# Attention and a SoLU block on one core: w_out handled by halves of its columns, four output tiles in halves, states in four loads, a new order

## The chip, the cores and the metric

The kernel runs on one core of a Trainium2 chip. The core has TensorE for matrix products (PE, with weight loads as PEld), VectorE (DVE), ScalarE (ACT), GpSimd (POOL) and SyncE (SP), which here issues all DMA transfers. Products land in PSUM; everything else lives in SBUF. The metric is the time of one execution on the device in microseconds. The profile is of one execution; a run's time is a little longer than the span from its first to its last instruction.

## What is computed

```python
# attention: x [8, 8, 512, 64], state [8, 8, 32, 64]
scores = scale * np.matmul(x, state.transpose(0, 1, 3, 2))
a = softmax(scores)
xread = np.matmul(a, state)
scores2 = scale * np.matmul(state, x.transpose(0, 1, 3, 2))
a2 = softmax(scores2)
sread = np.matmul(a2, x)
x = concatenate([xread, sread], axis=2)  # as 4352 rows of 512
# SoLU block: w_in [512, 1024], w_out [1024, 512], g_ln [1024]
h = x @ w_in
solu = h * softmax(h)
ln = (solu - mu) / np.sqrt(var + 1e-06) * g_ln
out = ln @ w_out
```

Both softmaxes run over the last axis; `mu` and `var` are those of a row of `solu`. All is float32.

## The kernel before, in words

The 4352 rows are 34 tiles of 128: four for each of eight batches, and tiles 32 and 33 for the state reads. Since `xread` is a product with the states, the kernel multiplies the states into w_in first (`state_w_in`, steps `V`: batch and half of the columns) and then takes h of a tile as softmax weights times that (`h_steps`, `H`). Products that need precision are made of three: each operand is split into a high part in a short float format and a low part (`swh` and `swl`, `ath` and `atl`, `uh` and `ul`, `wohi` and `wolo`), and high x high, high x low and low x high are summed. Batch 0 uses plain float32 operands in h.

A weight arrives as raw 64-bit words (`load_w`, `l`), 16 blocks: `l0` to `l7` are w_in, `l8` to `l15` w_out. ScalarE takes the rounding part (`low_words`, `cl`), VectorE shifts and masks in two operations, and a third operation adds the rounding (`to_f32`, `c`). w_in is used as it is for the states and, turned by small DMAs (`turn_w_in`, `wp`) and split (`split_w_in`, `wi`), for the last two tiles. w_out is split by `split_w_out` (`wo`): high part times g on ScalarE, low part times g on VectorE.

For a batch: load x (`LT`, `Ln`), scores (`S`), softmax over tokens (`E`), over states (`A`, for batch 0 in two parts `Ah`), reads (`R`). The products of w_in and the states of six batches are stored to DRAM (`Y`), loaded again when due (`Z`) and split (`P`). For a tile: h (`H`), the softmax and normalisation (`chain`, `C`: maximum, exponential, product, scaling, square), a transpose of blocks on VectorE, a store to DRAM and a rearranging load (`bounce`, `D`: tiles `ub`, `ut`, `back`), the split (`t_steps`, `T`), and the output product with eviction and store (`o_steps`, `O`): 24 products of 128x512, 48 of 128x256 for tile 33, whose two halves are made apart.

Nothing plans at run time. ORDER is a written list of steps; `issue` takes one piece of the named step per entry. OPT says which engine does the n-th piece of a kind (`a` ScalarE, `d` VectorE, `p` GpSimd). PLACES says which SBUF slot or PSUM bank the n-th tile of a kind gets; a tile that gets a slot waits for the last reader of the tile before it. Each engine then runs its own instructions in that order. SP is one queue too: a transfer that waits there holds up all behind it. `K` is one small product that only keeps TensorE busy.

Of the kernel before, what the change touches and what calls it, by code (L numbers as in the profile page):

```python
# [8 lines left out]
F32 = mybir.dt.float32  # L9
# [19 lines left out]
OPT = dict(ph=2, k4=45, direct=[0, 1], hn=[0], vh=[0, 1], ah=[0], add='dpdpdpdpppppppdp', whi='aadd', wlo='dppp',  # L29
           ev='daaaaaaaadaaadaaaaaaaaaaaaaaaaaa', swh='aaaaaaaaadaaaaaa', swl='pppppppppppdddpd', sub='dppddppd',  # L30
           subh='dpdddpdddpdddpdd', mulh='dddddpdddpdddpdd', mul='ppppdpdd', ath='aaaaaddd', alo='dpppppdp',
           up='aaaaaaaaddaaadaaaaaaaaddaadadadadd',
           uh='aaaaaaaadaaaddaaaaaaaaaaadaadaaadaaadaddaaaadaaddaaddadddadaaadadaaa',
           ul='ppddppppdpdppppppddppdppppddpppdpdpppdppppppppdppppdpppdddddppdddddd',
           oe='aaaaaaaaaaaaaadadaaaadadaaaaadaada', hs='aaaaaaaa', jit=[], ed=[0, 1], ec='aaaaaaaaaaaaaaaa')
# [36 lines left out]
C26 D26 O23*5 O24 R6*2 C27 C26 H28 D26 X D26 T27 C28 X C28*2 O25*3 H31 O25 O27 H31*2 O25*2 H31*2 O23 C28 D28*2 O25*4
O27*2 H31 D28 C25*2 T26 O25*2 T27 O25*2 T26*2 C31*2 H29*3 O27*3 wi2*2 O26 T26 H29*3 C31 O26*6 C31 D31*2 O27*2 O26 C26
O27*4 T28*4 C27 O28*3 O27*2 C28 O28*2 C29 O26*2 C29 O26*2 C29*2 D31 D29 C28 O28*2 T31*2 O28*3 T31*2 H30*4 O26 D29 O26
O28*2 H30*2 H33*3 C30 O31 O28 D29 C30*2 C31 C30*2 D30 O31*3 H33 wi1 H33*8 C33*3 H32 C31 H32*3 O31*3 C33 H32*3 D30*2
T30*3 D33 O31*4 O28 T29 O31*2 H32*4 D33*2 T29*2 H32 O31 C32*2 O30*2 O29*2 C32 T33 O29*3 O30 O29*3 C32 D32*3 O30*4
T33*2 O30*3 T30 O30*2 O29 C30 O30 C33 T29 O30 T33 O33*5 T32 O33*3 O29*3 T32 O33*3 T32 O33 C33 O33*9 O32*6 C29*2 O32*4
T32 O32*2 O33 O29*2 C32*2 O32*2 O33*6
# [25 lines left out]
def attention_then_solu_ffn(ctx, tc, xT, xn, stB, w_in, w_out, g, out):  # L104
# [11 lines left out]
    SLOTS = dict(s2=2, m1=1, z1=1, r=1, sc=2, rr=3)  # L116
# [52 lines left out]
    def load_st(k):  # L169

        st[k] = sbuf("s2", [P, 2 * NP * 2, 2, NS], F32, f"st{k}")
        nc.sync.dma_start(st[k].rearrange("p (k c s) h n -> p k c s (h n)", k=2, c=NP), stB[:, k:k + 2])
        yield

    def state_of(b, head):

        c, h = divmod(head, 2)
        return st[b // 4 * 2][h * D:(h + 1) * D, (b // 2 % 2) * 2 * NP + 2 * c + ((b % 2) ^ (c % 2)), h, :]
# [22 lines left out]
    def load_w(n):  # L201


        raw[n] = block([HALF, 2], U32, f"raw{n}")
        if n < 2 * NP:
            c, half = divmod(n, 2)
            src = w_in[c * P:(c + 1) * P, half * HALF:(half + 1) * HALF]
            nc.sync.dma_start(raw[n], src.bitcast(U32).rearrange("p (f k) -> p f k", k=2))
        else:
            src = w_out.bitcast(U32).rearrange("(p c f) h -> c f p h", p=4, f=NS)[n - 2 * NP]  # L210
            nc.sync.dma_start(raw[n].rearrange("p h k -> p (h k)"), src)
        yield
# [439 lines left out]
```

## Time and profile before

| | us |
|---|---|
| median of 3 runs | 352.25 (350.67 to 353.64) |
| the profiled execution's own time | 350.98 |
| its span | 349.2 |
| granted TensorE clock, mean | 0.995 |

The page gives busy times of each engine and the span in 40 slices; a digit is a tenth of a slice:

```profile
PE   5999999999999999999999999999999999999995
DVE  3889999997888778998779897888787896555720
ACT  3579999889658567578565676555863463544250
POOL 0063594378756764678579463444455518412220
PEclk9899999999999999999999999999999999999999
```

A busy TensorE is not one that does useful work all the time, since the small products of `K` and products that wait inside a group count as busy. So the useful products have to be counted. In an answer that lists instructions in order of time, a row has start, length, engine, line and operation, and in brackets the idle time before it with what ended it. The groups give busy time and the mean of one in ns.

### The profile page before, as it was taken

The numbers are of one execution on the slowest core, as the hardware profiler recorded it, in microseconds if no ns is written. First come the engines' busy times: TensorE is split into PE (matmuls) and PEld (weight loads), VectorE is DVE, ScalarE is ACT, GpSimd is POOL, SyncE is SP. The second block draws the span as 40 slices with busy tenths as digits, with TensorE's granted clock in tenths as the row PEclk, the third lists the DMA queues.
The fourth block names the chain that finished last, engine by engine and source line by source line (L and its number), as shares of the span: only waits on it lengthen the run. The fifth ranks groups of instructions, "written<-read, shape, count | busy, mean of one in ns | idle before, by whom it ended". The sixth has DMA issues, their size and how long they took to land.

```text
span 349.2 us, 6119 instructions
## 1 busy us (share of the span) xinstructions
PE 339.0 (97%) x2220; PEld 255.5 (73%) x2220; DVE 274.9 (79%) x386; ACT 220.6 (63%) x356; POOL 182.7 (52%) x241
## 2 busy tenths in 40 slices
PE   5999999999999999999999999999999999999995
PEld 4343335888788867888878778887888888888894
DVE  3889999997888778998779897888787896555720
ACT  3579999889658567578565676555863463544250
POOL 0063594378756764678579463444455518412220
PEclk9899999999999999999999999999999999999999
DMA  7996998899998899999997976897897345344432
GB/s 240 416 402 268 342 322 269 307 294 343 294 363 272 339 363 332 312 329 310 340 327 263 323 247 215 288 306 288 270 297 255 113 150 212 115 167 172 150 107 75
DMA packets 47854, 94.25 MB, mean 270 GB/s; under 512 B 4432, under 2 KB 26192, under 8 KB 47824
## 3 DMA queue, kind: packets, MB, share of 16 engines
q1 hardware_dynamic: 47824, 93.87, 77.8%
q8 instruction: 17, 0.28, 0.3%
q14 instruction: 13, 0.11, 0.1%
HBM read 54.53 MB, written 37.22 MB: 263 GB/s over the span
## 4 chain that ended last, share of the span: by engine, by line
PE 43%; DVE 20%; DMA 15%; ACT 11%; issue 4%; POOL 4%; SPq 1%; DVEq 0%; ACTq 0%; POOLq 0%
PE o L545 28%; PE h L477 13%; DMA back<-ut 7%; DMA out_dram<-osb 3%; DVE u L490 2%; DMA raw<-w_in_dram 2%; DVE sm L484 2%; ACT u L495 2%; DVE wf L234 2%; DVE ub L514 2%; ACT e L487 2%; ACT uh L142 2%; DMA ut<-ub 2%; POOL ul L147 1%; DVE aT L408 1%
## 5 line engine op out<-in xcount | busy, mean ns | idle before, releaser
L147 POOL TENSOR_TENSOR ul<-back,uh 128x512 fp32r<-128x512 f32 x43 | 58.8, 1373 | 66.4 <-ACT uh L142 40.1
L545 PE MATMUL o<-wohi,uh 128*128 128x512 f32 (+1 forms) x280 | 74.8, 385 | 0.6 <-ACT uh L142 0.4
L545 PE MATMUL o<-wolo,uh 128*128 128x512 f32 (+1 forms) x280 | 75.3, 383 | 0.0
L545 PE MATMUL o<-wohi,ul 128*128 128x512 f32 (+1 forms) x280 | 73.6, 383 | 0.0
L545 PEld LDWEIGHTS o<-wohi,uh 128*128 128x128 f32 x280 | 51.5, 188 | 12.1 <-ACT uh L142 1.3
L545 PEld LDWEIGHTS o<-wolo,uh 128*128 128x128 f32 x280 | 51.8, 188 | 10.4
L545 PEld LDWEIGHTS o<-wohi,ul 128*128 128x128 f32 x280 | 51.7, 188 | 10.3
L490 DVE SCALAR_TENSOR_TENSOR u<-h,e 128x1024 f32<-128x1024 f32 x34 | 41.4, 1217 | 22.1 <-ACT e L487 21.2
L487 ACT ACTIVATE e<-h,sm 128x1024 f32<-128x1024 f32 x34 | 37.9, 1113 | 29.0 <-DVE sm L484 28.7
L514 DVE STREAM_TRANSPOSE ub<-u 128x1024 f32<-128x1024 f32 x34 | 42.1, 1237 | 8.3 <-ACT u L495 7.9
L484 DVE TENSOR_REDUCE sm<-h 128x1 f32<-128x1024 f32 x34 | 41.0, 1207 | 8.5 <-PE h L477 4.6
L502 ACT ACTIVATE e<-u 128x1024 f32<-128x1024 f32 x34 | 35.9, 1056 | 9.5 <-DVE u L497 9.2
L142 ACT ACTIVATE uh<-back 128x512 fp32r<-128x512 f32 x48 | 29.0, 623 | 17.2 <-DMA back<-ut 17.2
L495 ACT ACTIVATE u<-u,sm 128x1024 f32<-128x1024 f32 x24 | 27.6, 1149 | 16.4 <-DVE u L490 16.3
L552 ACT ACTIVATE osb<-o,sm 128x512 f32<-128x512 f32 (+1 forms) x29 | 19.2, 663 | 25.4 <-PE o L545 12.1
L477 PE MATMUL h<-swh,ath 128*128 128x512 f32 x112 | 35.1, 395 | 0.0
L477 PE MATMUL h<-swl,ath 128*128 128x512 f32 x112 | 34.5, 389 | 0.0
L477 PE MATMUL h<-swh,atl 128*128 128x512 f32 x112 | 34.5, 389 | 0.0
L237 POOL TENSOR_TENSOR wf<-wf,r 128x512 uint32<-128x512 uint32 x11 | 14.0, 1290 | 27.7 <-DVE wf L234 23.9
L147 POOL TENSOR_TENSOR swl<-swf,swh 128x1024 fp32r<-128x1024 f32 x10 | 24.3, 2432 | 8.0 <-ACT swh L142 5.2
L477 PEld LDWEIGHTS h<-swh,ath 128*128 128x128 f32 x112 | 20.6, 188 | 5.3 <-ACT e L487 0.8
L477 PEld LDWEIGHTS h<-swl,ath 128*128 128x128 f32 x112 | 21.0, 188 | 4.5
(86 smaller groups left out, 496.8 us busy)
## 6 DMA issues: line engine op xcount, KB each, us to landing
ut<-ub SPq DMA_DIRECT2D x34, 512.0 KB, 3.1
back<-ut SPq DMA_DIRECT2D x34, 512.0 KB, 4.9
out_dram<-osb SPq DMA_DIRECT2D x33, 256.0 KB, 4.7
xT<-xT_dram SPq DMA_DIRECT2D x16, 512.0 KB, 8.0
xn<-xn_dram SPq DMA_DIRECT2D x16, 512.0 KB, 7.7
kept<-vt SPq DMA_DIRECT2D x12, 512.0 KB, 6.3
swf<-kept SPq DMA_DIRECT2D x12, 512.0 KB, 6.3
raw<-w_in_dram SPq DMA_DIRECT2D x8, 512.0 KB, 8.4
```

Source lines behind the costliest of these rows:

```text
L142: nc.scalar.activation(out, src, AF.Copy)
L147: engine(k).tensor_tensor(out=out, in0=a, in1=hi.bitcast(F32), op=ALU.subtract)
L237: engine(of("add", n)).tensor_tensor(out=w, in0=w, in1=rounding[n], op=ALU.add)
L477: nc.tensor.matmul(ph[t][:, cols], left[l][:, p, tok], weights[:, cols], start=(p, l, r) == (0, 0, 0), stop=(p, l, r) == (parts - 1, *kind ...
L484: nc.vector.tensor_reduce(nm, ph[t], AX.X, ALU.max, negate=True)
L487: nc.scalar.activation(e, ph[t], AF.Exp, bias=nm, accum_out=z)
L490: nc.vector.scalar_tensor_tensor(out=u, in0=ph[t], scalar=-1.0, in1=e, op0=ALU.mult, op1=ALU.mult, accum_out=su)
L495: nc.scalar.activation(u, u, AF.Identity, bias=su, scale=-float(DF))
L502: nc.scalar.activation(e, u, AF.Square, scale=float(DF) ** -0.5, accum_out=ss)
L514: nc.vector.transpose(ub, us[t][0])
L545: nc.tensor.matmul(po, ut[t][l][:, f, :], w[NP + f // 2][:, f % 2, cols], start=(hf, l, w is wohi, q) == (0, 0, True, 0), stop=(hf, l, q) ...
L552: nc.scalar.activation(o[:, cols], po, AF.Copy, scale=us[t][1])
```

## The change

Five things:

- The states are loaded in four transfers (256 KB each, one for two batches) in place of two of 512 KB.
- Each of the eight raw blocks of w_out holds half of the columns of two row chunks, in place of all columns of one; it takes two transfers of 256 KB. `l8` to `l11` are the first 256 columns, `l12` to `l15` the others.
- w_out's split is another: first a product with g in place (`wg`: five on VectorE, three on GpSimd), then the high part as a plain copy on ScalarE (`woh`), then the low part as a difference (`wol`: five on VectorE, three on GpSimd). Before, the products with g were part of the other two operations.
- Tiles 0 to 3 make their output in two halves of 256 columns, as tile 33 did. Each half has its own SBUF tile.
- ORDER, PLACES and the engine strings in OPT are new throughout. Counted over the kernel: VectorE adds in `to_f32` 5 to 9, GpSimd's 11 to 7; `uh` on ScalarE 48 to 32, VectorE 20 to 16, GpSimd 0 to 20; all evictions of the state products on ScalarE; `K` 34 to 33.

```diff
-    SLOTS = dict(s2=2, m1=1, z1=1, r=1, sc=2, rr=3)
+    SLOTS = dict(s4=4, m1=1, z1=1, r=1, sc=2, rr=3)
...
-        st[k] = sbuf("s2", [P, 2 * NP * 2, 2, NS], F32, f"st{k}")
-        nc.sync.dma_start(st[k].rearrange("p (k c s) h n -> p k c s (h n)", k=2, c=NP), stB[:, k:k + 2])
+        st[k] = sbuf("s4", [P, NP * 2, 2, NS], F32, f"st{k}")
+        nc.sync.dma_start(st[k].rearrange("p (c s) h n -> p c s (h n)", c=NP), stB[:, k])
...
-            src = w_out.bitcast(U32).rearrange("(p c f) h -> c f p h", p=4, f=NS)[n - 2 * NP]
-            nc.sync.dma_start(raw[n].rearrange("p h k -> p (h k)"), src)
+            half, i = divmod(n - 2 * NP, NP)
+            src = w_out.bitcast(U32).rearrange("(p c f) h -> c f p h", p=4, f=NS)
+            for c in range(2):
+                nc.sync.dma_start(raw[n].rearrange("p (c h) k -> p c (h k)", c=2)[:, c],
+                                  src[2 * i + c, :, :, half * DM:(half + 1) * DM])
...
-        w, by, hi, lo = wf[n][:, q], gT[:, f:f + 1], wohi[n][:, q], wolo[n][:, q]
-        if of("hs", f) == "a":
-            nc.scalar.activation(hi, w, AF.Copy, scale=by)
-        else:
-            nc.vector.tensor_scalar_mul(hi, w, by)
-        yield
-        nc.vector.scalar_tensor_tensor(out=lo, in0=w, scalar=by, in1=hi.bitcast(F32), op0=ALU.mult, op1=ALU.subtract)
+        w = wf[NP + m // 2][:, m % 2].rearrange("p (c h) -> p c h", c=2)
+        engine(of("wg", m)).tensor_tensor(out=w, in0=w, in1=gT[:, 2 * i:2 * i + 2, None].broadcast_to(w.shape), op=ALU.mult)
+        yield
+        hi, lo = (x[NP + i][:, :, half * DM // 2:(half + 1) * DM // 2] for x in (wohi, wolo))
+        copy(of("woh", m), hi, w)
+        yield
+        minus(of("wol", m), lo, w, hi)
...
-        width = DM // 2 if t == NTILES - 1 else DM
+        width = DM // 2 if t in OPT["oh"] else DM
...
-            if at == 0:
-                o = sbuf("o", [P, DM], F32, f"osb{t}")
+            o = sbuf("o", [P, width], F32, f"osb{t}_{at}")
```

Three places of the new order. In the rows a name has its tile or batch number and then a running number (`o1_0_737` is the output of tile 1 from column 0); the engine's rows stand in its order.

TensorE, where the first output product stands. Before, it comes behind h of tiles 4 and 5 (and the reads of batch 0 and the scores of batch 2, further up):

```order
L477 MATMUL h5_706<-swh1_1_439,ath1_660 128x512 x2
L477 MATMUL h5_706<-swl1_1_528,ath1_660 128x512 x2
L477 MATMUL h5_706<-swh1_1_439,atl1_688 128x512 x2
L545 MATMUL o1_0_737<-wohi4_680,uh1_730 128x512 x2
L545 MATMUL o1_0_737<-wohi5_683,uh1_730 128x512 x2
L545 MATMUL o1_0_737<-wolo4_681,uh1_730 128x512 x2
```

Now it comes behind the products of states of batch 7, and with h of tiles 4 and 5 still to do:

```order
L189 MATMUL swps7_1_1_600<-wf3_116,st3_467 32x512 x2
L572 MATMUL warm_92<-ident_74 128x128
L549 MATMUL o1_0_646<-wohi4_384,uh1_609 128x256 x2
L549 MATMUL o1_0_646<-wohi5_545,uh1_609 128x256 x2
L549 MATMUL o1_0_646<-wolo4_385,uh1_609 128x256 x2
L189 MATMUL swps6_0_1_655<-wf0_97,st3_467 32x512 x2
```

The first halves of tiles 1 and 0 moved ahead of h of tiles 4 and 5; their second halves follow it, and then tile 3.

VectorE up to and behind `ub` of tile 2, the last transpose of batch 0. Before, all of w_out's low parts lie ahead of it:

```order
L490 SCALAR_TENSOR_TENSOR u2_678,sm2_649<-h2_603,e2_676 128x1024
L271 SCALAR_TENSOR_TENSOR wolo5_684<-wf5_335,gT_81,wohi5_683 128x512
L234 SCALAR_TENSOR_TENSOR wf7_431<-raw14_366,wf7_431 128x512
L271 SCALAR_TENSOR_TENSOR wolo4_681<-wf4_397,gT_81,wohi4_680 128x512 x2
L271 SCALAR_TENSOR_TENSOR wolo5_684<-wf5_335,gT_81,wohi5_683 128x512
L237 ISA wf7_431<-wf7_431,r14_524 128x1024
L147 TENSOR_TENSOR ul1_732<-back1_658,uh1_730 128x512
L271 SCALAR_TENSOR_TENSOR wolo6_546<-wf6_269,gT_81,wohi6_545 128x512 x2
L271 SCALAR_TENSOR_TENSOR wolo7_743<-wf7_431,gT_81,wohi7_742 128x512
L147 TENSOR_TENSOR ul1_732<-back1_658,uh1_730 128x512
L271 SCALAR_TENSOR_TENSOR wolo7_743<-wf7_431,gT_81,wohi7_742 128x512
L514 STREAM_TRANSPOSE ub2_775<-u2_678 128x1024
```

Now the second halves of w_out are converted ahead of it, and their low parts come behind:

```order
L236 TENSOR_SCALAR wf7_246<-raw15_330 128x512
L239 SCALAR_TENSOR_TENSOR wf6_340<-raw13_441,wf6_340 128x512
L239 SCALAR_TENSOR_TENSOR wf7_246<-raw15_330,wf7_246 128x512
L242 ISA wf6_340<-wf6_340,r13_774 128x1024
L518 STREAM_TRANSPOSE ub2_784<-u2_731 128x1024
L440 TENSOR_TENSOR sr0_821<-srps0_788,sc0_178 128x128
L149 TENSOR_TENSOR wolo4_385<-wf6_340,wohi4_384 128x2x256
L149 TENSOR_TENSOR wolo5_546<-wf6_340,wohi5_545 128x2x256
L242 ISA wf7_246<-wf7_246,r15_724 128x1024
L270 TENSOR_TENSOR wf7_246<-wf7_246,gT_81 128x512
L149 TENSOR_TENSOR wolo6_462<-wf7_246,wohi6_461 128x2x256
```

The low parts of the first halves moved up, between the chains of tiles 1 and 0; those of the second halves moved behind the last `ub` of batch 0.

SP, where tiles 3 and 2 go through DRAM. Before, the load of tile 3 is ahead of the store of tile 2:

```order
L331 DMA ut3_715<-ub3_673 128x1024
L313 DMA swf2_0_727<-kept2_0_434 128x1024
L308 DMA kept5_0_755<-vt5_0_241 128x1024
L336 DMA back3_763<-ut3_715 128x4x256
L248 DMA wp2_781<-wf2_151 32x1024
L331 DMA ut2_797<-ub2_775 128x1024
```

Now it is behind it, and half an output stands there too:

```order
L335 DMA ut3_735<-ub3_733 128x1024
L312 DMA kept7_1_751<-vt7_1_584 128x1024
L561 DMA out_dram<-osb0_0_753 128x256
L335 DMA ut2_786<-ub2_784 128x1024
L340 DMA back3_836<-ut3_735 128x4x256
```

The load `back` of tile 3 moved behind a store that waits for the transpose of tile 2.

More of the change, by code (lines that the diff above doesn't have):

```diff
@@ L27 @@
 NTILES = B * NT + B * NS // P
[L29 to L35, printed above, removed]
@@ L78 @@
-T32 O32*2 O33 O29*2 C32*2 O32*2 O33*6
+OPT = dict(ph=2, k4=45, direct=[0, 1], hn=[0], vh=[0, 1], ah=[0], add='dddddpdpppdppdpd', whi='apdd', wlo='dpdd',
+           ev='aaaaaaaaaaaaaaaaaaaaaaaaaaaaaaaa', swh='aaaaaadaapapaada', swl='ppdppddppppdddpp', sub='dpddpdpp',
+           subh='dpdddpdddpdddpdd', mulh='dpdddpdddpdddpdd', mul='pdpppdpd', ath='aaaaapaa', alo='ddpppppp',
+           up='aaaaaaaadapdaaaaaadaadadaapdadaddd',
+           uh='aaaaaadapapppdaapaaaapaapaadpadpapddaappaapaaadppddapaddapddppadddap',
+           ul='dppdppdppdppdpddpdppppddpppdpdpppppdpppppppdpppdppdpppddddpdpdppdpdp',
+           oe='aaaaaaaaaadaaaaaaaaaaaaaaaaaddddaa', jit=[], ed=[0, 1], ec='aaaaaaaaaaaaaaaa', oh=[0, 1, 2, 3, 33],
+           wg='ddpddppd', woh='aaaaaaaa', wol='dppddddp')
@@ L177, in state_of @@
         c, h = divmod(head, 2)
[L178 removed]
+        return st[b // 2][h * D:(h + 1) * D, 2 * c + ((b % 2) ^ (c % 2)), h, :]
     def all_heads(b, banks, moving, js=range(NJ)):
@@ L257, in split_w_in, with split_w_out @@
         yield
-    def split_w_out(f):
-        n, q = NP + f // 2, f % 2
-        if q == 0:
-            wohi[n] = block([2, DM], F32R, f"wohi{n}")
-            wolo[n] = block([2, DM], F32R, f"wolo{n}")
-        w, by, hi, lo = wf[n][:, q], gT[:, f:f + 1], wohi[n][:, q], wolo[n][:, q]
-        if of("hs", f) == "a":
-            nc.scalar.activation(hi, w, AF.Copy, scale=by)
-        else:
-            nc.vector.tensor_scalar_mul(hi, w, by)
+    def split_w_out(m):
+        half, i = divmod(m, NP)
+        if half == 0:
+            wohi[NP + i] = block([2, DM], F32R, f"wohi{NP + i}")
+            wolo[NP + i] = block([2, DM], F32R, f"wolo{NP + i}")
+        w = wf[NP + m // 2][:, m % 2].rearrange("p (c h) -> p c h", c=2)
+        engine(of("wg", m)).tensor_tensor(out=w, in0=w, in1=gT[:, 2 * i:2 * i + 2, None].broadcast_to(w.shape), op=ALU.mult)
         yield
-        nc.vector.scalar_tensor_tensor(out=lo, in0=w, scalar=by, in1=hi.bitcast(F32), op0=ALU.mult, op1=ALU.subtract)
+        hi, lo = (x[NP + i][:, :, half * DM // 2:(half + 1) * DM // 2] for x in (wohi, wolo))
+        copy(of("woh", m), hi, w)
+        yield
+        minus(of("wol", m), lo, w, hi)
         yield
@@ L557, in o_steps @@
                 row = (t // NT) * ROWS + (t % NT) * P
-                nc.sync.dma_start(out[row:row + P, cols], o[:, cols])
+                nc.sync.dma_start(out[row:row + P, cols], o)
             else:
@@ L561, in o_steps @@
                 rows = out.rearrange("(b r) d -> r b d", r=ROWS)[S:, b:b + P // NS, cols]
-                nc.sync.dma_start(rows, o[:, cols])
+                nc.sync.dma_start(rows, o)
             yield
@@ L583, in attention_then_solu_ffn @@
         step(f"wo{f}", split_w_out, f)
-    for k in (0, 2):
+    for k in range(B // 2):
         step(f"Ls{k}", load_st, k)
```

102 lines of the change are left out of this document (52 added, 50 removed).

## The prediction

> **What bounds the kernel now.** I read the page first (busy shares, slices), then the windows, then the timeline of TensorE and VectorE in the first 75 us and the end.
>
> ```profile
> PE 339.0 (97%) x2220; PEld 255.5 (73%) x2220; DVE 274.9 (79%) x386; ACT 220.6 (63%) x356; POOL 182.7 (52%) x241
> ```
>
> The windows give, per stretch: its bounds and length, the busy time of each engine with its instructions, the granted clock, the DMA share.
>
> ```profile
> 0.00:19.50 19.50, 14.82 (x108) 7.89 (x112) 11.82 (x21) 7.91 (x11) 3.47 (x10) 0.91 0.90 337
> 19.50:57.40 37.90, 37.07 (x369) 14.40 (x359) 37.40 (x61) 35.81 (x63) 23.46 (x18) 1.00 0.88 325
> 0.00:68.70 68.70, 63.19 (x518) 31.66 (x519) 60.51 (x98) 54.35 (x92) 29.88 (x29) 0.98 0.89 323
> 63.00:345.20 282.20, 281.54 (x1729) 228.56 (x1727) 220.07 (x296) 171.48 (x275) 155.61 (x214) 1.00 0.76 260
> ```
>
> From 63 us on TensorE stands still for 0.66 us in 282: what lies there costs its own length and nothing can be gained but by fewer or shorter products. Before 57.4 us VectorE (37.40 of 37.90 after 19.5 us) and ScalarE (35.81) are the full ones, and TensorE's share is filled with single small products of `keep_warm` and late starts:
>
> ```profile
> 8.23 2.52 PE L187 MATMUL swph<-wf,st 64*32 64x512 f32 x8 [2.54 <-DVE wf L237]
> 18.37 1.19 PE L187 MATMUL sps<-xT,st 64*32 64x512 f32 x16 [0.80 <-ACT vt L142]
> 20.35 1.16 PE L569 MATMUL warm<-ident 128*128 128x128 f32 x8
> 25.17 1.38 PE L569 MATMUL warm<-ident 128*128 128x128 f32 x10
> 62.96 1.07 PE L545 MATMUL o<-wohi,uh 128*128 128x512 f32 x4
> 73.84 0.62 PE L545 MATMUL o<-wohi,uh 128*128 128x512 f32 x2
> ```
>
> The output products begin at 62.96 with tile 1. Tiles 1 and 0 are 48 products; 62.96 to 73.84 is 48 x 0.227. At 73.84 tile 3 begins. **This is my milestone**: by then TensorE has done every product of w_in with the states, the scores of batches 0 to 2, h of tiles 0 to 5, the reads of batch 0, and the output of tiles 1 and 0. The new order has exactly the same set of work ahead of tile 3's output (twice as many products for tiles 1 and 0, of half the width). What comes after is dense in both. So the forecast is: when does tile 3's output begin, plus what is added behind it.
>
> **The change part by part, against the profiled execution (350.98 us, span 349.2; the median of the runs is 352.25, 1.27 above it).**
>
> *VectorE up to the milestone.* In the window to 68.70 (the end of the fourth transpose `ub`, of tile 2) it is busy 60.51 and idle 8.2, of which 7.7 lie before 19.5 us. Prices:
>
> ```profile
> 11.90 1.29 DVE L237 CUSTOM_DVE_ANT_0 wf<-wf,r 128x1024 uint16<-128x1024 uint16 x2
> 61.90 0.68 DVE L237 CUSTOM_DVE_ANT_0 wf<-wf,r 128x1024 uint16<-128x1024 uint16 x1
> 62.50 0.68 DVE L147 TENSOR_TENSOR ul<-back,uh 128x512 fp32r<-128x512 f32 x1
> 63.11 2.07 DVE L271 SCALAR_TENSOR_TENSOR wolo<-wf,gT,wohi 128x512 fp32r<-128x512 f32 x3
> L147 DVE TENSOR_TENSOR swl<-swf,swh 128x1024 fp32r<-128x1024 f32 x4 | 4.8, 1198 | 0.0
> L144 DVE COPY vt<-swps 128x512 f32<-128x512 f32 x2 | 1.3, 681 | 0.0
> ```
>
> Back to back a 512-wide operation takes 0.6 (61.90 to 62.50 to 63.11), a `wolo` 0.67, a 1024-wide one 1.2. The fourth `ub` stands in the new order behind three more adds of `to_f32`, four products with g and two new low parts (9 x 0.6 = 5.4), one `swl` and one `atl` (2.4), and a wider product of the softmax (0.6); gone are eight `wolo` (8 x 0.67 = 5.4) and three evictions (2.0). Net +1.0: 61.5 of work. Behind it, five operations of 512 columns and a small one (3.3) end with the second-half low part of w_out's third block: 64.8.
>
> *Its idle time.* The first wait ends with the first landing and stays; others are landings, and the scores of batch 0:
>
> ```profile
> 4.70 0.43 DVE L231 TENSOR_SCALAR wf<-raw 128x512 uint32<-128x512 uint32 x1 [4.70 <-DMA raw<-w_in_dram]
> 5.94 0.43 DVE L231 TENSOR_SCALAR wf<-raw 128x512 uint32<-128x512 uint32 x1 [0.81 <-DMA raw<-w_in_dram]
> 9.57 0.43 DVE L231 TENSOR_SCALAR wf<-raw 128x512 uint32<-128x512 uint32 x1 [0.79 <-DMA raw<-w_in_dram]
> 19.50 1.44 DVE L388 STREAM_TRANSPOSE a<-sps 128x256 f32<-128x256 f32 x4 [1.11 <-PE sps L187]
> ```
>
> The new SP order has x of batch 0 two loads earlier and half the state bytes ahead of it. A 512 KB load takes about 1.24 us (4.70 to 5.94), so the scores can start some 3 us sooner (2 x 1.24 + 0.6), and the softmax fills what was idle. 4.7 stays, and a spacing of 512 KB loads that VectorE outruns early: I take 7.0 of idle, between 6.2 and the present 8.2. Then that low part ends at 64.8 + 7.0 = 71.8 (71.0 to 73.0). One product with g before it feeds the last block: ends 71.2, copy on ScalarE 0.6, difference on GpSimd 1.3 (next fence): 73.1. TensorE then has six rows of two 256-wide products left, 12 x 0.12 = 1.4: **74.5**, 0.7 later than 73.84.
>
> ```profile
> L147 POOL TENSOR_TENSOR ul<-back,uh 128x512 fp32r<-128x512 f32 x43 | 58.8, 1373 | 66.4 <-ACT uh L142 40.1 <-DVE uh L144 19.8 <-PE h L477 4.8
> 65.63 1.30 POOL L147 TENSOR_TENSOR ul<-back,uh 128x512 fp32r<-128x512 f32 x1 [8.04 <-ACT uh L142]
> 336.62 0.64 PE L545 MATMUL o<-wohi,uh 128*128 128x256 f32 x4
> 337.10 0.64 PE L545 MATMUL o<-wolo,uh 128*128 128x256 f32 x4
> ```
>
> *The second condition, SP's queue.* The load `back` of tile 3 now stands behind the store `ut` of tile 2, which waits for the fourth `ub` (61.5 + 7.0 = 68.5). From issue to landing the page has 4.9, so 73.5, and a conversion of 0.6: 74.1, just under 74.5.
>
> ```profile
> back<-ut SPq DMA_DIRECT2D x34, 512.0 KB, 4.9
> ```
>
> *Halves.* Four 256-wide products take 0.48 (336.62 to 337.10), 0.12 each against 0.1135 for half of 0.227. A tile in halves is 48 x 0.12 - 24 x 0.227 = +0.3; tiles 1 and 0 are in the milestone, tiles 3 and 2 add **+0.6**.
>
> *The end.* The last piece is now all 512 columns of tile 32; before it was 256 of tile 33.
>
> ```profile
> L552 ACT ACTIVATE osb<-o,sm x2: 473/474/475, 337.1 to 345.2; 128x256 f32<-128x256 f32 x2
> 332.16 0.69 ACT L552 ACTIVATE osb<-o,sm 128x512 f32<-128x512 f32 x1 [3.97 <-issue]
> DMA to landing us min/median/max: 2.0/2.2/2.5
> ```
>
> 0.2 for the eviction and up to 0.5 between a short and a long landing, 0.4 taken: **+0.6**.
>
> *What costs nothing.* State loads in four: half the bytes at a time, on a queue that runs ahead. Three transposing loads `wp` go into SP's queue between w_out's loads; they wait for the adds of two w_in blocks that are now GpSimd's first two operations, and what they hold up are loads that VectorE comes to later than they land. w_out's issues double; two of 0.54 fit into the 1.24 of a 512 KB load.
>
> ```profile
> L211 SPq DMA_DIRECT2D raw<-w_out_dram x8: 535/535/677, 10.8 to 22.4; - x8
> L395 POOL TENSOR_TENSOR a<-a,m 128x512 f32<-128x512 f32 x1 | 1.0, 1046 | 0.0
> ```
>
> Twenty conversions `uh` go to GpSimd, a price that no row has: from 0.43 (VectorE's) to 1.3 (GpSimd's two-input one), nearest GpSimd's 1.05 for a 512-wide difference; they lie under the distance from h to output.
>
> ```profile
> 322.39 0.61 PE L477 MATMUL h<-whi,xrl 128*128 128x512 f32 x2
> 335.55 0.43 DVE L144 CAST uh<-back 128x512 fp32r<-128x512 f32 x1 [4.86 <-DMA back<-ut]
> 336.01 1.29 DVE L147 TENSOR_TENSOR ul<-back,uh 128x512 fp32r<-128x512 f32 x2
> ```
>
> That way took 323.0 to 337.3, 14.3 us, at the end; the new order keeps 48 products of 512 and 48 of 256 there, 16.6 us, and the last second half is due 2 us later still.
>
> **Sum:** 350.98 + 0.7 + 0.6 + 0.6 = 352.9.
>
> **Rivals.** *Slower: VectorE waits for GpSimd.* Rows show the mechanism: a low part that takes 0.67 took 1.78 beside the GpSimd operation at 65.63, and a short operation (0.17 at 30.03) took 1.22 beside one at 46.56. With one more of that kind, some 2.9 us of VectorE's busy time up to the milestone is such blocking.
>
> ```profile
> 30.03 0.17 DVE L402 TENSOR_SCALAR z<-z 128x16 f32<-128x16 f32 x1
> 65.70 1.78 DVE L271 SCALAR_TENSOR_TENSOR wolo<-wf,gT,wohi 128x512 fp32r<-128x512 f32 x1
> 46.65 1.22 DVE L402 TENSOR_SCALAR z<-z 128x32 f32<-128x32 f32 x1
> 46.56 1.27 POOL L237 TENSOR_TENSOR wf<-wf,r 128x512 uint32<-128x512 uint32 x1
> ```
>
> The new order gives GpSimd three products with g and three low parts of w_out ahead of the milestone, and VectorE five products and five low parts in place of eight low parts. In my sum as many collide as now. If four more do, at about 1.1 each, the milestone is 4.4 later: 357.3. It decides from 3 us of blocking on; fewer adds on GpSimd (seven instead of eleven over the kernel) speak against it. The Trainium skill (SBUF — State Buffer, Who interferes with whom) has the rule: a VectorE instruction with two SBUF inputs contends with a GpSimd instruction that reads SBUF, and the later one waits until the first is done. The rows agree with it. If each of the six new pieces blocked VectorE for its whole 1.3, the sum would be 360.7; nothing here says that they all do.
>
> *Faster: VectorE is not what the milestone waits for.* If the new order keeps the two engines apart (2.9 us of blocking gone), idle time falls to its floor of 6.2 (0.8 less), and my row sums are 1 too high, the milestone is at 69.8 and the sum 348.2. Against it: ScalarE is as full, and the last weights hang on VectorE's count whatever TensorE does.
>
> *Slower, later:* tiles that now go through GpSimd come late, and TensorE's 0.66 of idle grows. Twenty conversions at 1.05 and what else moves give GpSimd some 25 us more on its 182.7, half its span; 5 us of it on the path would give 358.
>
> *No effect:* the output begins earlier with half the weights, and everything after waits for the other half. That is close to my forecast: earlier start, same milestone.
>
> **How the numbers follow.** Within 1% of the median shown (348.7 to 355.8; less than that a measurement of this kernel can hardly tell from no change): forecast and no-effect 0.66. Blocking 0.17 and late tiles 0.06: slower 0.23. Faster 0.11. Range: below, idle at its floor and all blocking gone, 352.9 - 0.8 - 2.9 = 349.2; above, four collisions, 357.3.
>
> **What would show it.** Right: output of tile 1 begins before 57 us, tile 3's between 73 and 76, TensorE idle under 2 us afterwards. VectorE's busy time to the fourth `ub` near 61.5. Wrong: VectorE rows of 1.2 to 1.8 us beside GpSimd ones; tile 3's output under 71 or over 77; gaps on TensorE after 80 us that end with `uh` or `ul` on GpSimd.

## The result and the profile after

| | before | after |
|---|---|---|
| median, 12 runs each, taken together | 353.14 us (350.67 to 356.50) | 356.90 us (354.68 to 358.62) |
| the profiled execution's own time | 350.98 | 354.93 |
| its span | 349.2 | 352.8 |
| ratio after to before | | 1.0102, 95% interval 1.0073 to 1.0131 |

The change made the kernel about 1% slower, just at the 1% that the prediction took as the bound between no change and slower; a ratio of 1 lies outside the interval. The forecast was 352.9 us; the time lies in the given range, near its upper end. Both profiles are of executions about 2 us faster than their kernels' medians, and the forecast was counted from the profiled 350.98: of the 4.0 us between 352.9 and 356.90, 2.2 are this base (353.14 - 350.98). The change itself was forecast at +1.9 and measured at +3.8 (medians) or +3.95 (profiles). Tile 1's output began 8 us sooner, and the whole kernel ended 4 us later.

The page of the kernel after, busy time of each engine:

```profile
PE 343.2 (97%) x2314; PEld 262.1 (74%) x2314; DVE 284.0 (80%) x384; ACT 209.2 (59%) x344; POOL 206.7 (59%) x267
```

Its windows (same columns as before: bounds, length, busy time of each engine, granted clock, DMA share, GB/s):

```profile
0.00:19.50 19.50, 15.31 (x110) 10.97 (x114) 12.88 (x23) 7.42 (x12) 3.54 (x9) 0.91 0.90 329
57.40:70.90 13.50, 12.80 (x146) 9.23 (x145) 12.39 (x17) 10.79 (x20) 4.93 (x4) 1.00 0.96 341
0.00:70.94 70.94, 65.52 (x532) 33.10 (x533) 62.62 (x98) 54.38 (x96) 29.65 (x37) 0.98 0.92 314
78.07:348.80 270.73, 270.60 (x1730) 222.10 (x1728) 215.76 (x277) 150.10 (x241) 175.55 (x228) 1.00 0.76 258
```

Its rows in order of time, those that answer to the steps of the prediction (engines mixed, many rows left out):

```profile
12.05 1.53 POOL L242 TENSOR_TENSOR wf<-wf,r 128x512 uint32<-128x512 uint32 x1 [10.76 <-DVE wf L239]
12.47 1.65 DVE L239 SCALAR_TENSOR_TENSOR wf<-raw,wf 128x512 uint32<-128x512 uint32 x1
...
26.46 1.29 POOL L242 TENSOR_TENSOR wf<-wf,r 128x512 uint32<-128x512 uint32 x1 [2.12 <-DVE wf L239]
26.61 1.42 DVE L236 TENSOR_SCALAR wf<-raw 128x512 uint32<-128x512 uint32 x1 [0.29 <-DMA raw<-w_out_dram]
...
54.98 0.72 PE L549 MATMUL o<-wohi,uh 128*128 128x256 f32 x4
...
60.58 2.43 POOL L149 TENSOR_TENSOR swl<-swf,swh 128x1024 fp32r<-128x1024 f32 x1
61.33 2.77 DVE L149 TENSOR_TENSOR atl<-aT,ath 128x1024 fp32r<-128x1024 f32 x1 [0.86 <-ACT ath L144]
65.16 1.23 DVE L518 STREAM_TRANSPOSE ub<-u 128x1024 f32<-128x1024 f32 x1
66.42 0.32 SPq L335 DMA_DIRECT2D ut<-ub  x1
...
68.13 1.10 PE L436 MATMUL srps<-xn,e 128*32 128x64 f32 x64 [0.70 <-DMA e<-e2d]
69.70 1.25 DVE L518 STREAM_TRANSPOSE ub<-u 128x1024 f32<-128x1024 f32 x1 [0.25 <-ACT u L499]
70.97 0.32 SPq L335 DMA_DIRECT2D ut<-ub  x1
72.13 0.37 SPq L340 DMA_DIRECT2D back<-ut  x1
73.56 0.68 DVE L149 TENSOR_TENSOR wolo<-wf,wohi 128x512 fp32r<-128x512 f32 x1
74.39 1.30 POOL L149 TENSOR_TENSOR wolo<-wf,wohi 128x512 fp32r<-128x512 f32 x1 [3.63 <-ACT wohi L144]
77.47 0.64 ACT L144 ACTIVATE uh<-back 128x512 fp32r<-128x512 f32 x1 [0.79 <-issue]
77.59 0.64 PE L549 MATMUL o<-wohi,ul 128*128 128x256 f32 x4
78.07 0.71 PE L549 MATMUL o<-wohi,uh 128*128 128x256 f32 x4
...
347.60 1.07 PE L549 MATMUL o<-wohi,ul 128*128 128x512 f32 x4
348.75 0.69 ACT L555 ACTIVATE osb<-o,sm 128x512 f32<-128x512 f32 x1 [4.23 <-PE o L549]
```

Read it from the end. Output of tile 3, the milestone of the prediction, begins at 78.07, before at 73.84. Behind it TensorE is as dense as it was: 270.6 us to the end of its last product (348.67), before 271.3 (73.84 to 345.12). The span ends 4.13 after the last product, before 4.08. So between these two profiles the whole loss lies ahead of the milestone:

| term | forecast | measured, profile against profile |
|---|---|---|
| milestone later | +0.7 | +4.2 (78.07 - 73.84) |
| TensorE behind it | +0.6 | -0.7 (270.60 - 271.28) |
| end | +0.6 | +0.05 |
| around the span | 0 | +0.35 (2.13 - 1.78) |
| sum | +1.9 | +3.95 |

Two things end together there. One is TensorE's own row: behind the wait of 0.70 at 68.13, for a load of batch 0's softmax (`e`), it has no gap up to the milestone and beyond; its last four products before it start at 77.59 and take 0.48, to 78.07. From the first output product at 54.98 on, TensorE is busy 22.39 of the 23.09 us.

The other is the way of tile 3: the transposed tile (`ub`, 65.16 to 66.39) is stored at 66.42, loaded again at 72.13 and converted from 77.47 on (e1 and e2 below show the start behind an idle gap that `uh` ends). How long store and load took from issue to landing:

```profile
L335 SPq DMA_DIRECT2D ut<-ub x1: 320/320/320, 66.4 to 66.4; - x1
DMA to landing us min/median/max: 5.7/5.7/5.7
...
L340 SPq DMA_DIRECT2D back<-ut x1: 370/370/370, 72.1 to 72.1; - x1
DMA to landing us min/median/max: 5.3/5.3/5.3
```

66.42 + 5.7 is 72.1, when the load is issued; 72.13 + 5.3 is 77.4. In the kernel before the same load was issued at 64.61 and took 5.4, so it landed at 70.0, nearly 4 us before its tile was due, and the last low part of w_out was done at 67.5 (65.70 and 1.78), 6 us before. There TensorE's own row alone set the milestone; now that row is later, and tile 3's way through DRAM and w_out's last low part (74.39 and 1.30: 75.7) have both come up to it.

### The profile page after: what moved, and what is told of

The parts are those of the page before. It is cut to its first block, busy times and chain, and to the rows that moved or that the text cites. A ratio compares the mean times of both kernels' runs of the same rounds, so it can differ in the third digit from the quotient of the medians.

```text
span 352.8 us, 6366 instructions
## 1 busy us (share of the span) xinstructions
PE 343.2 (97%) x2314; PEld 262.1 (74%) x2314; DVE 284.0 (80%) x384; ACT 209.2 (59%) x344; POOL 206.7 (59%) x267
## 3 DMA queue, kind: packets, MB, share of 16 engines
q1 hardware_dynamic: 49840, 93.87, 77.7%
## 4 chain that ended last, share of the span: by engine, by line
PE 91%; DMA 7%; ACT 1%; issue 0%; SPq 0%; ACTq 0%
PE o L549 52%; PE h L481 28%; PE swps L189 5%; DMA st<-stB_dram 3%; PE srps L436 2%; DMA e<-e2d 2%; PE sps L189 2%; DMA raw<-w_in_dram 1%; PE swph L189 1%; PE warm L572 1%; ACT swf L144 0%; ACT osb L555 0%; ACT a L401 0%; ACT r L225 0%; ACT vt L144 0%
## 5 line engine op out<-in xcount | busy, mean ns | idle before, releaser
L549 PE MATMUL o<-wolo,uh 128*128 128x512 f32 (+1 forms) x312 | 77.4, 363 | 0.0
L549 PE MATMUL o<-wohi,ul 128*128 128x512 f32 (+1 forms) x312 | 76.1, 362 | 0.0
L549 PEld LDWEIGHTS o<-wolo,uh 128*128 128x128 f32 x312 | 54.7, 189 | 10.9 <-POOL wolo L149 0.8
L549 PEld LDWEIGHTS o<-wohi,ul 128*128 128x128 f32 x312 | 54.8, 189 | 9.3
L549 PEld LDWEIGHTS o<-wohi,uh 128*128 128x128 f32 x312 | 54.6, 188 | 9.3 <-POOL uh L146 0.2
L555 ACT ACTIVATE osb<-o,sm 128x512 f32<-128x512 f32 (+1 forms) x34 | 21.0, 621 | 39.5 <-DMA out_dram<-osb 15.8
L499 ACT ACTIVATE u<-u,sm 128x1024 f32<-128x1024 f32 x22 | 25.4, 1153 | 17.4 <-DVE u L494 17.3
L146 POOL CAST uh<-back 128x512 fp32r<-128x512 f32 x20 | 12.5, 627 | 36.7 <-DMA back<-ut 24.5
L144 ACT ACTIVATE uh<-back 128x512 fp32r<-128x512 f32 x32 | 19.6, 630 | 18.0 <-DMA back<-ut 17.0
L481 PEld LDWEIGHTS h<-swh,atl 128*128 128x128 f32 x112 | 20.7, 188 | 4.6 <-DVE atl L149 0.3
```

The lines of the kernel that those rows point to most:

```text
L144: nc.scalar.activation(out, src, AF.Copy)
L481: nc.tensor.matmul(ph[t][:, cols], left[l][:, p, tok], weights[:, cols], start=(p, l, r) == (0, 0, 0), stop=(p, l, r) == (parts - 1, *kind ...
L499: nc.scalar.activation(u, u, AF.Identity, bias=su, scale=-float(DF))
L549: nc.tensor.matmul(po, ut[t][l][:, f, :], w[NP + f // 2][:, f % 2, cols], start=(hf, l, w is wohi, q) == (0, 0, True, 0), stop=(hf, l, q) ...
L555: nc.scalar.activation(o, po, AF.Copy, scale=us[t][1])
```

## The experiments

Theories, as the expectations name them. V: VectorE is late, blocked by GpSimd, and the last low parts of w_out with it. T: TensorE's own row from its first output product on is the limit. S and R: tile 3's way through DRAM, its load or the whole trip. D: tile 0's load. L: tiles whose `uh` is made on GpSimd come late. All ratios are to the kernel before, on the same chip; that of the change is 1.0102 (1.0073 to 1.0131). First the milestones, all from profiles (`ub` end, store issue and landing, load issue and landing are those of tile 3). A profile is one execution, so a few tenths between two of them mean little:

| kernel | `ub` end | store | load | last low part | milestone | from there to TensorE's end |
|---|---|---|---|---|---|---|
| before | 57.5 | 57.5, 64.6 | 64.6, 70.0 | 67.5 | 73.84 | 271.3 |
| after | 66.4 | 66.4, 72.1 | 72.1, 77.4 | 75.7 | 78.07 | 270.6 |
| e1 | 67.1 | 67.1, 71.6 | 72.1, 77.9 | 76.3 | 78.53 | 272.1 |
| e2 | 66.8 | 66.9, 70.3 | 71.8, 77.8 | 76.3 | 78.41 | 273.0 |
| e3 | 66.2 | 66.2, 70.8 | 71.1, 76.0 | 75.7 | 77.30 | 271.9 |
| e4 | 67.9 | 67.9, 72.3 | 72.9, 77.6 | 77.2 | 78.79 | 271.1 |
| e5 | 65.2 | 65.3, 73.0 | 73.0, 77.5 | 74.5 | 78.14 | 272.5 |
| e6 | 65.9 | 65.9, 73.4 | 73.4, 77.7 | 75.2 | 78.42 | 277.3 |
| e9 | 64.2 | 64.8, 71.1 | 71.4, 77.6 | 76.6 | 78.28 | 270.6 |
| e10 | 65.2 | 65.3, 72.0 | 72.1, 76.5 | 75.7 | 77.31 | 272.8 |
| e11 | 63.4 | 64.1, 70.5 | 70.6, 76.6 | 75.7 | 77.49 | 271.3 |

**e1: one low part from GpSimd to VectorE**

```diff
-           swl='ppdppddppppdddpp'
+           swl='ppddpddppppdddpp'
```

> The changed kernel with one letter changed: the fourth low part of the kept state products (swl of batch 1, second half) goes from GpSimd, where it ran from 60.58 to 63.01 us, to VectorE. Theory V (VectorE is what the output of tile 3 waits for; it came late because GpSimd blocked it): the operation atl at 61.33 takes 1.2 instead of 2.77, for one more operation of 1.2 that fills the 0.86 of idle, so all VectorE work behind it is about 1.1 earlier: tile 3's output at 77.0 instead of 78.07, time 355.8 against 356.9. Theory T (TensorE itself is full from its first output product at 54.98 on, and its own pieces set the end): 356.9, tile 3's output at 78.1, whatever VectorE gains. Theory S (tile 3's load back, landed at 77.4, sets it): back 1.1 earlier, as V.

356.78 us, ratio 1.0105 (1.0071 to 1.0138): no change. VectorE's rows of this kernel:

```profile
60.25 0.69 DVE L149 TENSOR_TENSOR ul<-back,uh 128x512 fp32r<-128x512 f32 x1 [1.17 <-ACT uh L144]
...
62.18 1.50 DVE L149 TENSOR_TENSOR swl<-swf,swh 128x1024 fp32r<-128x1024 f32 x1
63.60 1.21 DVE L149 TENSOR_TENSOR atl<-aT,ath 128x1024 fp32r<-128x1024 f32 x1
```

The blocking is gone (`atl` 1.21 in place of 2.77), and the time with it went into the added operation (1.50) and into a wait for tile 0's `uh`, whose load landed at 59.5 here and at 57.5 in the profile of the change. So the largest collision was exchanged for as much work: VectorE wasn't earlier (`ub` of tile 3 ends at 67.1, in the change at 66.4), and V is not put to the test by this run. Tile 3's output begins behind a gap of 0.43 that `uh` ends, as S expects.

**e2: TensorE's row closed up; e3: that and e1's edit** (pieces of long lines of ORDER; two entries of PLACES that change places with them are left out)

```diff
-V71 V70 K Y51
+V71 V70 Y51
-Ln00 K O1*2
+Ln00 O1*2
-V61 O1*4 T1 E0 C3 P10 T0*2 O1 V61
+O1*3 V61*2 O1 T1 E0 C3 P10 T0*2 O1
-H4*2 D2*2 R0*3 S2 wo5 H5 D3 Y50 O0 H4*2 H5 wo4
+H4*2 D2*2 wo5 H5 D3 Y50 O0 H4*2 H5 R0*3 S2 wo4
```

> The changed kernel with TensorE's row closed up between 52 and 72 us, nothing else: two idle-filling products (K) taken out ahead of the first output product, the two halves of the last state product of batch 6 put side by side (apart they take 0.99 us each, side by side 1.0 for both), the read of batch 0 and the scores of batch 2 put behind six rows of h, so that the 0.7 wait for e2 is filled. Theory T: some 2.0 to 2.4 us less on TensorE, tile 3's output near 76, time 354.8. Theory V: the last low parts of w_out (done at 75.7) and uh of tile 3 hold it: 356.9. Theory S: tile 3's uh waits for its load, landed at 77.4, so 78.1 and 356.9, with TensorE idle just ahead of tile 3's output.

> Both edits together (the low part on VectorE, and TensorE's row closed up). T: as the second alone, 354.8. V: as the first alone, 355.8. If the two limits are about equal, so that each alone hides the other: clearly less than either alone, 354.8 to 355.8, with each alone near 356.9.

e2: 357.18, ratio 1.0104 (1.0067 to 1.0141). e3: 356.85, ratio 1.0109 (1.0071 to 1.0148). In e2 TensorE made its first output product at 53.34, 1.6 sooner, and then stood idle. Its waits from 50 to 79 us, in total, times, longest, and its row at the milestone:

```profile
PE h L481 <- DVE atl L149: 1.3, 1, 1.3
PE o L549 <- POOL ul L149: 0.5, 1, 0.5
PE o L549 <- DVE uh L146: 0.3, 1, 0.3
PE o L549 <- ACT wohi L144: 0.2, 1, 0.2
```

```profile
78.41 0.71 PE L549 MATMUL o<-wohi,uh 128*128 128x256 f32 x4 [0.30 <-DVE uh L146]
```

So T alone falls for e2: the gap has only moved, and its last piece waits for `uh` of tile 3, as S expects. One of the two pairs of state products gave less than expected, too: 1.89 (55.75 to 57.64) in place of 1.0, since the weights of its second half waited 0.74 for an eviction on ScalarE. e3's milestone is the only one of the first four that is earlier (77.30), by less than hoped, and its time doesn't show it. In e3 the load (76.0) is there well before, and TensorE has no gap from 68 on: here its own row ends last.

**e4: tiles 2 and 3 whole again**

```diff
-oh=[0, 1, 2, 3, 33]
+oh=[0, 1, 33], ow=[2, 3]
...
+        if t in OPT["ow"]:
+            yield from o_whole(t)
+            return
```

`o_whole` makes the 24 products of 512 columns into one bank, one eviction and one store; every second of its steps is empty.

> The changed kernel with the second product of tiles 2 and 3 in one piece of 512 columns (their steps kept at the places of the halves, every second one empty). If a product of 256 columns costs 0.12 against half of 0.227, this takes 0.3 per tile off TensorE's dense part: 356.3 against 356.9. If the halves hide in waits: 356.9.

355.44 (12 runs), ratio 1.0073 (1.0050 to 1.0096). The difference to the change is -0.29% with about 0.37% of uncertainty either way, from the two intervals: the expected -0.6 us fits, and so does nothing. Not settled by time.

**e5 and e6: transfers in SP's row moved**

```diff
-Y51 T1*2 wo3*2 C3 A1 T1 wo2 wp2 D0 Y40
+T1*2 wo3*2 C3 A1 T1 wo2 D0 Y51 wp2 Y40
```

and for e6 also

```diff
-H4*2 D2*2 R0*3 S2 wo5 H5 D3 Y50
+H4*2 D2 D3 D2 R0*3 S2 wo5 H5 Y50
```

> The changed kernel with two steps of SP's row moved, nothing else: the store of a kept state product (Y51) and four loads of wp, issued at 49.15 and 49.59 between the store ut of tile 0 and its load back, now stand behind that load. Theory D (a DMA round trip holds the stage: in three of the last four profiles ScalarE and VectorE stand still for 0.6 to 1.6 us until back of tile 0 lands at 58.6 to 59.5): back of tile 0 lands 1 to 1.5 us earlier (near 56.2 to 57.5), no wait for it, 355.6 against 356.9. Theory V (the VectorE work ahead of the last low parts of w_out alone): 356.9, the same milestone of 78 to 78.5.

> As the one before, and the load back of tile 3 ahead of the store ut of tile 2 in SP's row. Theory S (the load back of tile 3, landed at 77.4 to 77.9, sets the start of its output): it lands about 1.3 earlier (near 76.2), tile 3's output starts about 1 us earlier, 354.8 to 355.2. If the last low parts (done at 75.7) and TensorE's own row are as late: as the one before, 355.6.

e5: 357.36, ratio 1.0131 (1.0089 to 1.0173). With nothing put between store and load, tile 0's load was issued at 53.5, when its store had landed (48.91 + 4.6), and still took 4.4; in the change it was issued at 53.0 and took 4.5. What stood between them had not held it up. The trip isn't any shorter, so this doesn't test whether the trip holds the stage (D).

```profile
L340 SPq DMA_DIRECT2D back<-ut x1: 371/371/371, 53.5 to 53.5; - x1
DMA to landing us min/median/max: 4.4/4.4/4.4
```

e6: 359.96, ratio 1.0203 (1.0155 to 1.0250), 0.7% slower than e5; the six times of the one all lie above the six of the other. SP's row:

```profile
65.91 0.32 SPq L335 DMA_DIRECT2D ut<-ub  x1
...
73.42 0.37 SPq L340 DMA_DIRECT2D back<-ut  x1
73.88 0.46 SPq L335 DMA_DIRECT2D ut<-ub  x1
```

The load of tile 3 can't be issued before its store has landed (73.4). The store of tile 2, ready at 70.4, now stands behind this waiting load, 2.9 us later than in the change, and tile 2's load lands at 83.1 in place of 80.2. Tile 3 gained nothing and tile 2 lost: behind the milestone TensorE's row takes 277.3 (in an execution of 361.79, the longest of the six; the waits listed there add up to 3.0 us, and the rest of the 6.7 more than in the change is not accounted for).

**e7: all edits so far together (e3, e4, e6)**

> All edits so far in one kernel: SP's row as in the last one, TensorE's row closed up, the low part on VectorE, tiles 2 and 3 whole. If each of the three limits (VectorE's work, TensorE's row, the loads) hides the others, only this one moves: 353.5 to 354.5, with the output of tile 3 near 76. If the set of VectorE and ScalarE work ahead of the milestone is the limit: 355.5 to 356.3 (the tiles in whole alone give some 0.6).

359.24, ratio 1.0182 (1.0133 to 1.0231). Both expectations fall; e6's edit is in it, and nearly e6's time. Its milestone is 78.06.

**e8: the kernel before, scores of batch 2 later**

```diff
-R0 V61 D1 A1 S2 C3 D3
+R0 V61 D1 A1 C3 D3
-H5 wo5 H5*3
+H5 wo5 H5*3 S2
```

> The kernel before with one step moved: TensorE does the scores of batch 2 behind h of tiles 4 and 5 in place of ahead of them. Theory T for the kernel before (TensorE is full from 57.4 on and its row alone sets tile 3's output at 73.84; the low parts are done at 67.5): the scores no longer wait 0.83 us for the evicted read of batch 0 and h starts up to 2 us sooner; tile 3's output at 72.4 to 72.8, time 1.0 to 1.4 less. Theory V for it (VectorE, full from 57.4 to 73.8 as well, sets it): no change.

352.81 (12 runs), ratio 0.9989 (0.9954 to 1.0023): no change. TensorE stands still for what it passed:

```profile
58.46 0.74 PE L477 MATMUL h<-swh,atl 128*128 128x512 f32 x2 [0.82 <-POOL atl L147]
```

Tile 3's output begins at 75.29 in this profile, not at the 72.4 to 72.8 of T. So before, too, the engines ahead of TensorE are close behind it. None of the twelve kernels is faster than the one before.

**e9, e10, e11: on e3, tile 3's transpose early; two low parts on GpSimd; both**

```diff
-P11 O0*3 C2 A1 C3 A1 O0 cl15 Y41 O1*2 C2 D3*2
+P11 O0*3 C2 C3 A1 D3 A1 O0 cl15 Y41 O1*2 C2 D3
-wol='dppddddp'
+wol='dppdppdp'
```

(The first two lines are e9, with the slots of `ub` of tiles 2 and 3 exchanged; the last two e10; e11 has both.)

> The kernel with both edits (low part on VectorE, TensorE's row closed up; 356.85, tile 3's output at 77.3 in its profile) with one thing more: on VectorE the transpose ub of tile 3 stands ahead of atl and of u of tile 2, on ScalarE its u ahead of ath, and ub of tiles 2 and 3 exchange their buffers, so that this can be. ub of tile 3 ends about 2.3 us earlier (66.2 to 63.9). Theory R (the round trip of tile 3, from ub over its store and its load to uh, 11 to 12 us, sets the start of its output): load back lands near 74, tile 3's output near 75.3, time 354.8. Theory V (the last low parts of w_out, done at 75.6, and what TensorE does behind them set it): 77.3 and 356.9, with uh of tile 3 waiting for nothing.

> The kernel with both edits, with two letters more: the second-half low parts of w_out's first two blocks go from VectorE (71.0 to 72.3) to GpSimd, idle from 70.6 to 74.4. Theory V: VectorE's last operations for w_out are 1.2 earlier, the last low part is done at 74.5, tile 3's output at 76.1 to 76.7 (then its load, landed at 76.0, holds it), time 355.7 to 356.3. Rival (GpSimd blocks VectorE's two-input operations at 72.2 to 73.5, 1.0 to 1.2 us each, as the operation atl was): no gain or up to 1 us later, 356.9 to 357.9.

> Both additions together. If the round trip of tile 3 and the last low parts of w_out are each a limit at 77: tile 3's output at 75.3 to 76, 354.8 to 355.5, clearly less than either alone. If one of them alone is: as that one.

e9: 357.47, ratio 1.0135 (1.0095 to 1.0176). e10: 356.63, ratio 1.0097 (1.0065 to 1.0130). e11: 356.76, ratio 1.0096 (1.0063 to 1.0128). e9 did what it should to VectorE, and SP's row shows why it wasn't enough:

```profile
64.78 0.46 SPq L335 DMA_DIRECT2D ut<-ub  x1
...
70.95 0.32 SPq L335 DMA_DIRECT2D ut<-ub  x1
71.38 1.16 SPq L340 DMA_DIRECT2D back<-ut  x1
```

`ub` of tile 3 ends 2.0 us earlier than in e3, on which e9 is built, and its store is issued 1.4 earlier, but lands 0.3 later (71.1 for 70.8). From 57.4 to 70.9 the DMA engines are full (share 0.99 in e9); that this is why is not shown. Then the load is issued right behind the store of tile 2 (70.95), takes 6.2 and lands at 77.6. Taking away the load's place behind that store (e6), or the late producer (e9), gave nothing alone; both together were not tried.

An earlier load would not have been enough in e9, though. The operations that stepped back for `ub`, `ath` on ScalarE and `atl` on VectorE, now hold TensorE:

```profile
63.50 0.74 PE L481 MATMUL h<-swh,ath 128*128 128x512 f32 x2 [0.46 <-ACT ath L144]
...
65.34 0.74 PE L481 MATMUL h<-swh,atl 128*128 128x512 f32 x2 [0.62 <-DVE atl L149]
```

Behind these waits its row runs without a gap to the milestone at 78.28, 1.0 later than in e3. In e11 TensorE waits at the same places (0.45 and 0.58), and its output of tile 3 begins at 77.49, no earlier than in e3 or e10.

e10 shows the other rival at work. GpSimd's two low parts take 1.5 each in place of 1.3, and VectorE's operations beside them 1.15 and 1.66 in place of 0.68:

```profile
69.35 2.99 POOL L149 TENSOR_TENSOR wolo<-wf,wohi 128x512 fp32r<-128x512 f32 x2
70.05 1.15 DVE L242 CUSTOM_DVE_ANT_0 wf<-wf,r 128x1024 uint16<-128x1024 uint16 x1
71.23 1.66 DVE L270 TENSOR_TENSOR wf<-wf,gT 128x512 f32<-128x512 f32 x1
```

What VectorE was spared (1.2) came back as blocking (1.4); the last low part is done at 75.7 as in e3, and here it is what TensorE's row waits for. The Trainium skill (SBUF — State Buffer, Who interferes with whom) says that a VectorE instruction with two SBUF inputs contends with GpSimd's reads. These rows agree, and the one-input operation at 26.61 (1.42, alone 0.43) belongs to the operations that the same section lets contend in a faster mode; whether it ran in one isn't shown.

**e12: the conversions of GpSimd on ScalarE**

```diff
-uh='aaaaaadapapppdaapaaaapaapaadpadpapddaappaapaaadppddapaddapddppadddap'
+uh='aaaaaadaaaaaadaaaaaaaaaaaaadaadaaaddaaaaaaaaaadaaddaaaddaaddaaadddaa'
```

> The changed kernel with the twenty conversions uh of GpSimd on ScalarE in place of it. Theory L (tiles through GpSimd come late: TensorE idles 0.6 to 1.8 us near 97 in four profiles, ended by uh of GpSimd): 355.4 to 356.0. Theory R (that tile's load back is late, whoever converts): the idle time near 97 stays, within 0.3, ended by ScalarE: 356.9. If ScalarE's added 13 us delay its own work: above 357.5.

368.75, ratio 1.0429 (1.0380 to 1.0479). The third case holds, with more than was expected, and hides whatever L would have given. In its profile (an execution of 372.22) TensorE waits 10.1 us in two places for `uh` on ScalarE, 8.2 of it in one. In the change GpSimd makes these conversions at 0.63 each:

```profile
L146 POOL CAST uh<-back 128x512 fp32r<-128x512 f32 x20 | 12.5, 627 | 36.7 <-DMA back<-ut 24.5
```

Where a tile is late, the profiles show the load late, not the engine. In e5 GpSimd waits 2.31 us for tile 4's load, and TensorE 1.77 for GpSimd:

```profile
96.45 0.61 POOL L146 CAST uh<-back 128x512 fp32r<-128x512 f32 x1 [2.31 <-DMA back<-ut]
97.12 1.20 PE L549 MATMUL o<-wohi,uh 128*128 128x512 f32 x4 [1.77 <-POOL uh L146]
```

The profiles of e1 (1.10), e3 (1.20), e4 (0.65) and e7 (2.03, where GpSimd's own wait ends with another load) have this wait too; those of the change, e2, e9 and e11 have not. Whether the usual execution of the change pays it isn't shown.

## Why the prediction was right in range and low

- **The class and the milestone.** That the output begins early and nothing is won was right: tile 1's output at 54.98 (forecast: before 57), and the end is set by when tile 3's begins. The milestone was mis-sized: 74.5 forecast, 78.07 measured, beyond the 77 named as wrong. This is the step that failed: both of its conditions came later than forecast, and a third, TensorE's own row, was put at nothing.
- **TensorE's own row** (no term in the forecast, which counts only six rows of products behind the last low part). "The same set of work ahead" is true, but of that work 22.39 us now lie behind the first output product: the output of tiles 1 and 0 (96 products of 0.12, 11.5), h of tiles 4 and 5, the read of batch 0, the scores of batch 2 and the last products of the states. From 54.98 on, this row ends near 77.4 even without its one wait of 0.70; for 74.5 it would have had to start near 52. With the row as it is packed here, the forecast's sign for tile 3, 76 at the latest, needs a start by 53.6; its sign for tile 1 would have let it start as late as 57. In e3, e9 and e11 this row ends last: no gap stands ahead of their milestones (77.30, 78.28, 77.49).
- **VectorE to the fourth `ub`** (forecast 61.5 of work and 7.0 of idle, 68.5): 62.6 and 8.3, 70.94. Work is 1.1 more, of it some 0.6 blocking: the rows at 12.47, 26.61 and 61.33 are 3.5 longer than the same operations alone (0.68, 0.43, 1.21), where 2.9 were taken. Idle time is 1.3 more, just above the range given: the early start before 19.5 us came (6.6 idle in place of 7.7), but 1.1 of new waits stand between 57.4 and 70.9.
- **From there to the last low part** (forecast 3.3 and 1.3): 3.3 (74.25) and 1.4 (75.7). Right. With e4's and e10's 1.6 from the last low part to the milestone this condition alone gives 77.3.
- **Tile 3's load in SP's queue** (forecast: issued with the store of tile 2 at 68.5, landed 4.9 later, 74.1 with the conversion): this was called the second condition, just under the first, and of the two it ended last, together with TensorE's row. The store of tile 2 came at 70.97 (+2.5). The load wasn't issued with it but at 72.13 (+1.2), when tile 3's own store landed, 5.7 after its issue; the forecast had no term for that store. The load took 5.3 (+0.4). Together 78.1. The diff's row showed the load behind a store; it took the table above to see that the load waits for tile 3's own store as well.
- **Halves.** Four 256-wide products take 0.48, as forecast. TensorE behind the milestone is nevertheless 0.7 shorter, not 0.6 longer: it stood still for 0.58 us there before (270.70 busy of 271.28), now not at all. That is 0.6 of the 1.3 between forecast and measurement; the rest is not accounted for. e4 leaves the price unsettled.
- **The end** (forecast +0.6): the eviction of 512 columns took 0.69 in place of 0.47, but the span ends 4.13 behind the last product in place of 4.08. The landing term was wrong.
- **What costs nothing.** The early loads did start the scores sooner: the first idle stretch is shorter. The conversions on GpSimd cost 0.63 each, not 1.05; e12 shows that with them on ScalarE the kernel loses 4%.
- **The slower rival** (VectorE blocked by GpSimd, 357.3) has the measured time and not the measured cause: blocking grew by 0.6, not by 4.4. That the time lies in the range, whose upper end this rival set, is luck as far as the cause goes. Of the two rows that the prediction took for the contention of two SBUF inputs, only the one at 65.70 has two; the one at 46.65 reads one tile. The late-tiles rival is half right: tile 4's load comes late near 97 us in four profiles of near kernels (e1, e3, e4, e5), and GpSimd waits for it.

The limits on the milestone stand within about 1 us of each other: TensorE's row, the last low part and 1.6, the load and 0.65. Edits of one met another (e2, e9, e10) or didn't make it earlier (e1, e5, e6). Where the 4 us lie is read from the profiles; no edit won them back, so which limit to move first, and by how much it would help, stays open.

## What to carry to other kernels

When a step that was the last to arrive is moved forward, list everything that the next dense stage needs and when each arrives: what had 4 us of slack becomes the limit. For data that goes through DRAM and back, count the store too: the load is issued when the store has landed, and both wait their turn in a queue. Moving only one of the load's place and its producer brought nothing here (e6, e9), and moving both was not tried. A waiting load in a single queue also holds up stores that are ready (e6, 0.7% lost). And add up the row of the engine that does the dense work, from its first moved piece to the milestone: here that sum alone, 22.4 us, ruled the forecast out.

## What the runs showed of the hardware

- Issuing a store earlier hardly landed it earlier while the DMA share was 0.96 to 1.01 (57.4 to 70.9 us, the change and e1 to e4): over the variants tile 3's store was issued between 64.1 and 67.9 and landed between 70.3 and 73.4, in no order with its issue.
- A rearranging 512 KB load took 4.4 us with nothing put between it and its store (e5, tile 0), that of tile 3 4.3 to 6.2 over the variants.
- GpSimd's conversion of 128x512 takes 0.63 us, VectorE's 0.43, ScalarE's 0.64 by the row at 77.47: a copy with one input is as cheap on GpSimd as on ScalarE, while its difference of two inputs takes 1.30, against 0.68 on VectorE.
- Products of the states (64 rows x 32 columns of weights) can cost as much in pairs as alone: in the change a step of eight records takes 0.99 (52.33 to 53.32, where the next product starts). In the kernel before, two such steps start together at 48.80, sixteen records, and the next product starts at 49.82: 1.02 for both. The new order leaves more of them apart. A pair gains only where both halves can start: of e2's two pairs one took 1.02 (52.32 to 53.34), the other 1.89, with a wait of 0.74 inside. e2's time shows that closing this row alone wins nothing.
